# Moving 1.5 MB of one gradient store to four of the sixteen DMA engines in a one-query attention kernel

## The chip, the cores and the metric

The kernel runs on one core of one Trainium2 chip. The metric is the device time of one execution in microseconds. Before the change it is 646.4 us, the median of three runs (646.16 to 646.51). The profile of one execution has a span of 644.5 us at a mean granted TensorE clock of 0.600.

## The reference

It is attention with one query per head, forward and backward, for 32 heads, 8192 keys and a head size of 128, all bf16. The outputs are the attention result and the gradients of q, k and v.

```python
B, H, Sq, Skv, Dh = 1, 32, 1, 8192, 128
scores = jnp.einsum('bhqd,bhkd->bhqk', q, k) * q.shape[-1] ** -0.5
attn   = jax.nn.softmax(scores, axis=-1)
out    = jnp.einsum('bhqk,bhkd->bhqd', attn, v)
# out, and the gradients of q, k, v for a given grad_out (jax.vjp)
```

K and V of one head are 2 MB each, and so are dK and dV. The kernel has to read 134.23 MB and write 134.23 MB, and does little arithmetic with either.

## The kernel before

The kernel goes head by head. Every transfer that matters here is issued on the sync queue (SP). A head is kept with 128 partitions of 64 rows each, so that a full store or load is 128 packets of 16 KB. It has 16 landings, one for each DMA engine, and on the first engine the landings of successive transfers are 4.85 to 4.87 us apart (564.21, 569.08, 573.93, 578.80, 583.65 us), which is eight packets of 607 ns. K and V come in ahead of their use:

```python
def load_v(h):
    Vt[h] = vpool.tile([P, NT, D], BF16, tag="V", name="Vt")
    nc.sync.dma_start(Vt[h][:], rows_of(v, h, 0, 1))
```

dK and dV are outer products of one value for each key and one row. VectorE makes them in four quarters (`r` = 0 to 3) in a buffer `G` in SBUF; the store is issued after the last quarter, or in two halves for the first and the last head:

```python
def outer(h, which, r):
    # ... (cut: choice of the operands; Q = NT // 4)
    nc.vector.tensor_tensor(slots(G, r, 4)..., op=ALU.mult)      # shortened
    parts = 1
    if h == 0 or h == H - 1:
        parts = 2
    if r % (4 // parts) == 4 // parts - 1:
        c = r // (4 // parts)
        nc.sync.dma_start(rows_of(dst, h, c, parts), slots(G, c, parts))
```

`G` has two buffers for each of dK and dV, so a store has to land before the product of the head after the next one may overwrite it.

## Time and profile before

| What | Value |
|---|---|
| Time | 646.4 us |
| Span of the profile | 644.5 us |
| Busy: TensorE, VectorE, ScalarE | 75%, 78%, 28% |
| Bytes in bulk transfers, all on the sync queue's hardware queue | 268.47 MB |
| DMA rate with all engines busy | about 428 GB/s |
| Last landing of the last big store: first engine, last engine | 633.9 us, 643.22 us |

Three kinds of record are used. The page's row of slices cuts the span in 40 equal parts and gives the DMA engines' mean busy share in tenths and the GB/s. The view of stretches (windows) gives, for each stretch of time, the busy time and instruction count of TensorE, its weight loads, VectorE, ScalarE and GpSimd, then the granted TensorE clock, the DMA share and the GB/s. Below these lie the raw records: each DMA packet with its start, size and duration, and each increment of a semaphore. A store raises its semaphore once for each engine that takes part, when this engine's part has landed: 16 times for a full store. These "landings" show how far the engines are apart, though neither kind of record names the engine.

### The profile page before, as it was taken

What the parts mean: (1) busy time and instruction counts of PE and PEld (TensorE: products, weight loads), DVE (VectorE), ACT (ScalarE), POOL (GpSimd) and SP (SyncE); (2) the same over time, 40 slices, a digit from 0 to 9 for tenths busy, and PEclk for the clock granted to TensorE, in tenths of its full rate; (3) what the DMA queues carried; (4) which work ended last, traced back from release to release, by engine and by line L of the source; (5) the groups of instructions that cost most, each with busy time, mean ns of one, the idle gap of its engine ahead of it and who ended that gap; (6) DMA issues with size and microseconds to landing.
All of it is one profiled execution on the core that took longest, in us unless ns stands there. A gap on an engine that the chain in (4) does not pass through costs nothing.

```text
span 644.5 us, 20935 instructions
## 1 busy us (share of the span) xinstructions
PE 481.0 (75%) x9673; PEld 452.0 (70%) x9673; DVE 505.5 (78%) x653; ACT 183.5 (28%) x332; POOL 0.7 (0%) x6
## 2 busy tenths in 40 slices
PE   3898888886677877768777787667786777877780
PEld 2888888886677866768666777667785676866670
DVE  5989899867977779777788777797767977778860
ACT  2333333332233222233222332223322223222230
POOL 0000000000000000000000000000000000000000
PEclk9766666655666655666556666556655666655665
DMA  8999999999999999999999999999999999999985
GB/s 349 407 425 430 424 425 423 429 426 431 427 428 427 427 427 429 429 429 425 433 422 433 425 430 427 427 429 425 427 429 425 431 425 429 429 427 430 424 365 238
DMA packets 19718, 269.80 MB, mean 419 GB/s; under 512 B 2352, under 2 KB 2352, under 8 KB 2864
## 3 DMA queue, kind: packets, MB, share of 16 engines
q1 hardware_dynamic: 19584, 268.47, 98.2%
q8 instruction: 75, 1.23, 0.7%
q14 instruction: 11, 0.09, 0.0%
q10 hardware_dynamic: 48, 0.01, 0.0%
HBM read 134.23 MB, written 134.23 MB: 417 GB/s over the span
## 4 chain that ended last, share of the span: by engine, by line
DMA 59%; PE 21%; DVE 14%; ACT 2%; issue 1%; SPq 0%; DVEq 0%; ACTq 0%
DMA Kt<-in_k_dram 48%; DVE XK_sb L146 8%; PE T_ps L183 8%; DMA out_dram<-G_dv 5%; DMA out_dram<-G_dk 5%; PE s_ps L157 5%; DVE G_dk L210 4%; PE dp_ps L200 3%; PE m_ps L200 2%; PE dp_ps L195 2%; ACT XT_sb L185 1%; PE m_ps L294 1%; DVE G_dv L210 1%; PE s_ps L173 1%; DVE sm L163 1%
## 5 line engine op out<-in xcount | busy, mean ns | idle before, releaser
L210 DVE TENSOR_TENSOR G_dv<-p_rep,qd 128x2048 bf16<-128x2048 bf16 x128 | 148.2, 1221 | 90.3 <-DMA out_dram<-G_dv 84.6
L183 PE MATMUL T_ps<-ident_f,Vt 128*128 128x128 f32 x1024 | 203.4, 382 | 0.2 <-PE m_ps L294 0.2
L183 PEld LDWEIGHTS T_ps<-ident_f,Vt 128*128 128x128 f32 x1024 | 190.7, 210 | 0.2 <-issue 0.2
L185 ACT COPY XT_sb<-T_ps 128x1024 f32<-128x1024 f32 x128 | 128.6, 1013 | 129.3 <-PE T_ps L183 127.2
L210 DVE TENSOR_TENSOR G_dk<-ds_rep,qd 128x2048 bf16<-128x2048 bf16 x128 | 155.6, 1218 | 2.9 <-DMA out_dram<-G_dk 1.9
L146 DVE STREAM_TRANSPOSE XK_sb<-Kt 128x1024 f32<-128x1024 f32 x128 | 148.3, 1214 | 5.8 <-DMA Kt<-in_k_dram 4.7
L157 PEld LDWEIGHTS <-XK_sb 128*128 128x128 bf16 x2048 | 57.7, 104 | 90.7 <-DVE pdt L234 79.9
L157 PE MATMUL s_ps<-q_blk,XK_sb 128*128 128x4 bf16 x2048 | 59.7, 168 | 82.1 <-DVE pdt L234 72.1
L195 PE MATMUL dp_ps<-do_blk,XT_sb 128*128 128x2 bf16 x2048 | 66.7, 164 | 18.1 <-ACT XT_sb L185 18.1
L195 PEld LDWEIGHTS <-XT_sb 128*128 128x128 bf16 x2048 | 64.9, 102 | 20.7 <-ACT XT_sb L185 20.7
L200 PE MATMUL dp_ps<-ds_rep,Kt 128*128 128x1 bf16 x2048 | 64.1, 165 | 1.3 <-issue 1.0
L200 PEld LDWEIGHTS <-Kt 128*128 128x128 bf16 x2048 | 59.6, 104 | 6.8 <-issue 6.6
L244 ACT COPY dq_all<-dp_ps 128x1 f32<-128x1 f32 x32 | 5.1, 159 | 192.4 <-PE dp_ps L200 178.5
L200 PEld LDWEIGHTS <-Vt 128*128 128x128 bf16 x2048 | 57.7, 97 | 0.9
L200 PE MATMUL m_ps<-p_rep,Vt 128*128 128x1 bf16 x2048 | 56.9, 164 | 0.0
L294 PEld LDWEIGHTS m_ps<-rs,ones_f 128*128 128x128 f32 x64 | 16.0, 311 | 49.9 <-ACT e L293 49.9
L294 PE MATMUL m_ps<-rs,ones_f 128*128 128x1 f32 x64 | 18.8, 362 | 40.5 <-ACT e L293 40.5
L303 ACT ACTIVATE p_rep<-e,rinv 128x256 bf16<-128x256 f32 x32 | 16.3, 508 | 30.1 <-DVE rinv L301 30.1
L163 DVE TENSOR_TENSOR sm<-s_ps,in_quad 128x256 f32<-128x256 f32 x32 | 13.6, 424 | 11.1 <-PE s_ps L157 7.9
L229 ACT CAST qd<-s_ps 128x256 bf16<-128x256 f32 x32 | 11.9, 372 | 32.2 <-PE s_ps L225 32.2
L236 DVE SCALAR_TENSOR_TENSOR ds_rep<-dp_ps,pdt,p_s 128x256 bf16<-128x256 f32 x32 | 15.5, 484 | 5.2 <-PE dp_ps L195 2.4
L293 ACT ACTIVATE e<-s_ps,nbias 128x64 f32<-128x64 f32 x32 | 10.0, 313 | 31.8 <-DVE nbias L290 31.8
(44 smaller groups left out, 143.4 us busy)
## 6 DMA issues: line engine op xcount, KB each, us to landing
Vt<-in_v_dram SPq DMA_DIRECT2D x32, 2048.0 KB, 30.0
Kt<-in_k_dram SPq DMA_DIRECT2D x31, 2048.0 KB, 30.8
out_dram<-G_dv SPq DMA_DIRECT2D x30, 2048.0 KB, 34.6
out_dram<-G_dk SPq DMA_DIRECT2D x30, 2048.0 KB, 33.6
out_dram<-G_dv SPq DMA_DIRECT2D x4, 1024.0 KB, 15.0
out_dram<-G_dk SPq DMA_DIRECT2D x4, 1024.0 KB, 13.3
Kt<-in_k_dram SPq DMA_DIRECT2D x4, 512.0 KB, 5.1
out_dram<-fin_sb SPq DMA_DIRECT2D x2, 8.0 KB, 13.1
```

The costliest lines, as they stand in the source:

```text
L146: nc.vector.transpose(XK[h][:, :, :, u, :], slots(Kt[h], u, NCH).rearrange("p g d -> p (g d)").bitcast(F32).rearrange("p (g w j) -> p g w ...
L157: nc.tensor.matmul(out[:, g, :], lhsT=cols[:, g, c // 2, c % 2], rhs=q_blk[:, h, c, :], start=(c == 0), stop=(c == 2 * NB - 1), skip_group ...
L163: nc.vector.tensor_tensor(x["sm"][:], x["s"][:, 0:NT].rearrange("p (a g) -> p a g", a=NQ).unsqueeze(2) .to_broadcast([P, NQ, NCH, CH]), in ...
L183: nc.tensor.transpose(T_ps[:, i, :], words[:, m * P:(m + 1) * P], ident_f[:])
L185: nc.scalar.copy(X[:], T_ps[:])
L195: nc.tensor.matmul(st[h]["dp"][:, n:n + 2], lhsT=X[:, i, e2, :], rhs=do_blk[:, h, e2, :], start=(e2 == 0), stop=(e2 == 1), skip_group_chec ...
L200: nc.tensor.matmul(out_col, lhsT=Xt[:, n, :], rhs=rep[:, n, 0:1], start=(n == 0), stop=(n == NT - 1), skip_group_check=True)
L210: nc.vector.tensor_tensor(slots(G, r, 4).rearrange("p n (a b) -> p n a b", b=R), slots(rep, r, 4).unsqueeze(2).to_broadcast([P, Q, D // R, ...
L229: nc.scalar.copy(x["qd"][:].rearrange("p a d -> p (a d)"), x["s"][:, 256:512])
L236: nc.vector.scalar_tensor_tensor(out=x["ds"][:], in0=x["dp"][:, 0:NT].unsqueeze(2).to_broadcast([P, NT, R]), scalar=pdt[:], in1=x["p_s"][: ...
L294: nc.tensor.matmul(x["m"][:, 0:1], lhsT=ones_f[:], rhs=rs[:], start=True, stop=True, skip_group_check=True)
L303: nc.scalar.activation(x["p"][:], e[:].unsqueeze(2).to_broadcast([P, NT, R]), ACT.Copy, scale=rinv[:])
```

## The change

The intent is to even out the DMA engines at the end of the kernel. Nine of them end late and seven end early; the change takes work for one store from twelve engines and gives it to four. The first quarter of dV of head 30 (0.5 MB) still goes out on all 16 engines. The other three quarters (1.5 MB) go out as one store of 124 partitions and one of 4. The change counts on both using the same four engines. No trace before the change showed this. Their numbers, 0 to 3, are in no record and serve only as names: in e3 the landings of loads of 1, 2, 4 and 8 partitions tell the engines apart, and "engine 3" is one that takes part in a load of four partitions but not in one of two.

```diff
-        if r % (4 // parts) == 4 // parts - 1:
+        if h == H - 2 and which == "dv":
+
+            rows4 = dst[0, h].rearrange("(p n) d -> p n d", p=P)
+            if r == 0:
+                nc.sync.dma_start(rows4[:, :Q, :], G[:, :Q, :])
+            elif r == 3:
+                for lo, hi in ((0, P - 4), (P - 4, P)):
+                    nc.sync.dma_start(rows4[lo:hi, Q:, :], G[lo:hi, Q:, :])
+        elif r % (4 // parts) == 4 // parts - 1:
             c = r // (4 // parts)
             nc.sync.dma_start(rows_of(dst, h, c, parts), slots(G, c, parts))
```

## The prediction

> **What bounds the kernel now.** I read the row of 40 slices first, then the queues, the issues of the sync queue, the stretches of the last 40 us, and last the landing times.
>
> From the page (slices, then queues):
>
> ```profile
> DMA  8999999999999999999999999999999999999985
> GB/s 349 407 425 430 424 425 423 429 426 431 427 428 427 427 427 429 429 429 425 433 422 433 425 430 427 427 429 425 427 429 425 431 425 429 429 427 430 424 365 238
> ...
> q1 hardware_dynamic: 19584, 268.47, 98.2%
> q8 instruction: 75, 1.23, 0.7%
> q14 instruction: 11, 0.09, 0.0%
> ```
>
> The DMA engines are full from the second slice to the 38th at about 428 GB/s; no compute engine is over 78% busy. So the time is the bytes over the DMA rate, plus a tail in the last two slices (365 and 238 GB/s). 428 GB/s over 16 engines is 26.7 GB/s each. The packet records agree: a 16 KB packet takes 611 ns and the next begins 4 ns before it ends, so 607 ns each (27.0 GB/s); in the same way 8 KB costs 305 ns and 4 KB 155 ns.
>
> The sync queue's last issues in order of time (start us, us, engine, line, what):
>
> ```profile
> 594.00 0.33 SPq L220 DMA_DIRECT2D out_dram<-G_dk  x1
> 602.61 0.33 SPq L220 DMA_DIRECT2D out_dram<-G_dv  x1
> 614.52 0.33 SPq L220 DMA_DIRECT2D out_dram<-G_dk  x1
> 621.05 2.60 SPq L220 DMA_DIRECT2D out_dram<-G_dv  x2
> ...
> 627.72 2.60 SPq L220 DMA_DIRECT2D out_dram<-G_dk  x2
> ```
>
> These are dK of head 29, dV of head 30 (the store that is changed), dK of 30, the two halves of dV of 31 and of dK of 31. No load is left behind them. After 627.7 us nothing but stores remains:
>
> ```profile
> 612.00:616.00 4.00, 2.64 (x12) 2.33 (x12) 2.90 (x6) 1.07 (x4) 0.00 (x0) 0.50 0.74 311
> ...
> 636.00:640.00 4.00, 0.00 (x0) 0.00 (x0) 0.00 (x0) 0.00 (x0) 0.00 (x0) 0.50 0.55 232
> 640.00:645.00 5.00, 0.00 (x0) 0.00 (x0) 0.00 (x0) 0.00 (x0) 0.00 (x0) 0.50 0.09 37
> ```
>
> The last two columns are DMA share and GB/s. A share of 0.55 is about 9 of 16 engines busy: the engines do not end together, and 7 are done while 9 still work.
>
> The landing records say the same more sharply. A store raises its semaphore once for each of the 16 engines, so each has 16 landing times. For dK of head 29 the first comes at 607.96 us, six more 0.03, 0.18, 0.24, 0.50, 1.53 and 4.91 us later, then a gap, and nine from 12.73 to 15.43 us later. Early in the run all 16 lie within 0.6 us. The lag grows by about 1.5 us on one engine at each packet of queue 8 (takes about 1.02 us, and the packet behind it about 1.1 instead of 0.61). Followed packet by packet, these 75 fetches go round eight engines; the ninth late engine has none and falls behind slowly, by packets of 620 to 700 ns. The last landing of dK of 31 is at 633.9 us on the first engine and at 643.22 us on the last; the span ends at 644.5 us and the run counts 646.4. So the nine late engines set the end, and they never idle on the way.
>
> [...]
>
> **Which engines lead?** The records do not name them. Where two packets of different size or duration start in the same nanosecond, their order in the record is stable (one pair 12 times of 12), and in nearly all such pairs a leading engine stands before the late one without fetches, and this before the fetching ones. If the records are kept by engine number, the fetching ones are 8 to 15 and the leaders among 0 to 7. I take it that 0 to 3 lead; an inference, at some 88%.
>
> **The change part by part.**
>
> The computation is untouched: every instruction of the compute engines stays, in the same order. The sync queue gets three issues (128 x 4 KB after the first quarter, some 3.4 us earlier; 124 x 12 KB; 4 x 12 KB) for one. Nothing in the tail waits for dV of head 30: dV of 31 needs the buffer of dV of 29, dK of 31 that of dK of 29. So issue times stay.
>
> Twelve engines: they had 8 packets of 16 KB (8 x 607 = 4.86 us) of dV of 30 and now have 8 of 4 KB (8 x 155 = 1.24 us): minus 3.62 us each. The late ones have no idle time before the end, so all of it arrives: 643.22 - 3.62 = 639.6 us.
>
> Engines 0 to 3: 1.24 us plus 31 + 1 = 32 packets of 12 KB. At (305 + 607)/2 = 456 ns, an estimate between 8 and 16 KB, that is 14.59 us; together 15.83 instead of 4.86 us. A first engine free of dK of 29 at 607.96 ends dV of 30 at 623.8, dK of 30 (4.86) at 628.7, dV of 31 (16 x 305 = 4.88) at 633.5 and dK of 31 (4.88) at 638.4 us. Before, it idled between these and ended at 633.9: of the 10.97 us added, about 6.5 go into gaps. With the leaders' lags of 0 to 1.53 us they end at 638.4 to 639.9, beside the late ones' 639.6.
>
> Sum: the end moves from 643.2 to about 639.6 to 639.9, and 646.4 becomes 642.8 to 643.1: 0.5% faster. The size of 1.5 MB is just the balance of the two groups, so more should not be hoped for.
>
> **The rivals.**
>
> *A lagging leader is among 0 to 3.* One leader is 4.91 us late. On 0 to 3 it would end at 638.4 + 4.9 = 643.3: no change, 646.5. By count alone 4 in 7; the balance of the size speaks against it, so I give it less.
>
> *Shared ports.* [...] Two readers at one port, if each gets half, take 2 x 456 ns a packet: 14 us more at worst, end near 652, time 650 to 656; with three at one port, up to 664. [...] I give it 3 in 10.
>
> *The four engines are late ones.* Then all 10.97 us fall on the end: 654.2, time 657.4. One in ten.
>
> *The compute chain or the sync queue takes over.* The chain ends at 630 us with the last issue; a half of dK of 31 needs 2.44 us and the landing, so it cannot end before about 634. It leaves 5 us of room.
>
> **Range and chances.** The mechanism worked out gives 642.8 to 643.1; the rivals lie on the upper side alone, so I put the point a little above, at 643.6 us. Below, nothing can go under 639.6 - 643.2 by more than noise, hence 642.3. Above, the ports and the wrong engines could reach 664; 657 leaves out about one in ten. Faster by over 2% (under 633.5) would need more than the whole tail of the late engines: 1%. Slower by over 2% (over 659.3) is the worst of the port rival: 9%. Within 2%: 90%.
>
> **What would show it.** Right: the store of 124 partitions lands in about 16 to 20 us after its issue with 4 landings, its 12 KB packets take about 460 ns, the last stretch has nearly all 16 engines busy until 639 us and then falls off steeply, and the late engines end about 3.6 us sooner. Wrong by ports: 12 KB packets of 600 to 1300 ns and 16 KB ones well over 611 at the same time, and four engines alone at work after 641 us. Wrong by the engines' place: 12 KB packets at 460 ns, yet four engines alone to 654 us. Wrong altogether: 16 landings for the 124-partition store, and the time of before.

The sum: 643.22 - 3.62 = 639.6 us for the late engines, up to 639.9 for the four, with 646.4 - 643.2 = 3.2 us from the last landing to the time, so 642.8 to 643.1 us. But that just four engines take the 32 packets, and that the same four serve both stores, stands in it as an assumption, and so does the "port" of the rival: the word names a theory, that reads of SBUF by several engines can slow each other. No record shows a port.

## The result, and the profile after

The changed kernel takes 654.33 us, the median of four runs (653.93 to 654.78), against 646.28 us (646.16 to 646.51, four runs) for the kernel before. The ratio is 1.0124, with a 95% interval of 1.0107 to 1.0142. Ratios here are the mean time of one kernel's runs over that of the other's of the same rounds, so not quite the ratio of the medians that are quoted. The kernel became 1.2% slower.

The page's slices of the kernel after:

```profile
DMA  8999999999999999999999999999999999999992
GB/s 347 410 426 424 426 426 425 430 426 429 426 430 425 430 427 429 424 430 428 429 426 431 427 429 428 428 429 425 429 426 430 427 429 426 429 426 430 378 335 102
```

Up to the 37th slice nothing has changed (a slice is 16.3 us here and 16.1 before). The last three fall to 378, 335 and 102 GB/s (before: 424, 365 and 238), although the busy share stays at 90% or more in slices 38 and 39. The engines are busy and move less.

The sync queue's issues of the kernel after (start us, us, engine, line, what):

```profile
599.42 0.33 SPq L222 DMA_DIRECT2D out_dram<-G_dv  x1
602.83 0.82 SPq L225 DMA_DIRECT2D out_dram<-G_dv  x2
614.00 0.36 SPq L228 DMA_DIRECT2D out_dram<-G_dk  x1
620.87 2.68 SPq L228 DMA_DIRECT2D out_dram<-G_dv  x2
...
627.09 3.02 SPq L228 DMA_DIRECT2D out_dram<-G_dk  x2
```

These are the first quarter of dV of head 30, its two stores on four engines, dK of 30, and the halves of dV and dK of 31. Each comes within 0.7 us of its place before (602.61, 614.52, 621.05, 627.72). So the computation was not held up, and the loss came after the issues, on the DMA engines.

More stretches of the kernel before:

```profile
616.00:620.00 4.00, 4.00 (x37) 3.94 (x36) 1.34 (x2) 2.32 (x3) 0.00 (x0) 0.50 1.03 438
...
628.00:632.00 4.00, 0.00 (x0) 0.00 (x0) 1.96 (x2) 0.25 (x1) 0.00 (x0) 0.50 0.94 395
...
640.00:644.00 4.00, 0.00 (x0) 0.00 (x0) 0.00 (x0) 0.00 (x0) 0.00 (x0) 0.50 0.11 46
```

The same stretches, and the later ones, of the kernel after:

```profile
612.00:616.00 4.00, 2.70 (x14) 2.67 (x14) 2.38 (x5) 1.15 (x4) 0.00 (x0) 0.50 0.87 351
616.00:620.00 4.00, 4.00 (x59) 3.97 (x58) 1.52 (x2) 2.69 (x3) 0.00 (x0) 0.64 1.00 374
...
628.00:632.00 4.00, 0.00 (x0) 0.00 (x0) 1.33 (x2) 0.00 (x0) 0.00 (x0) 0.50 0.98 340
...
636.00:640.00 4.00, 0.00 (x0) 0.00 (x0) 0.00 (x0) 0.00 (x0) 0.00 (x0) 0.50 0.60 251
640.00:644.00 4.00, 0.00 (x0) 0.00 (x0) 0.00 (x0) 0.00 (x0) 0.00 (x0) 0.50 0.25 105
644.00:648.00 4.00, 0.00 (x0) 0.00 (x0) 0.00 (x0) 0.00 (x0) 0.00 (x0) 0.50 0.16 66
648.00:652.00 4.00, 0.00 (x0) 0.00 (x0) 0.00 (x0) 0.00 (x0) 0.00 (x0) 0.50 0.05 21
```

The last two columns, DMA share and GB/s, are to be read together. From 616 to 620 us all engines are busy in both kernels, yet they move 438 GB/s before and 374 after. From 628 to 632 us the share rises from 0.94 to 0.98 while the rate falls from 395 to 340. From 640 to 644 us the share is 0.25, which is 4 of 16 engines; then it falls to 0.05, which is one engine.

The packet records of the two new stores, worked out from the trace, say the same packet by packet:

```text
128 packets of 12 KB, mean 693 ns
  the 28 that start before 613.3 us          460 ns each
  the 39 that start from 613.3 to 619 us     mean 578 ns
  the 61 that start after 619 us             mean 872 ns, up to 1966 ns
16 KB packets in the same time               up to 1276 ns (before: up to 1019; most 611)
first 12 KB packet of the four engines       608.48, 608.74, 610.18, 613.99 us
```

And the landings, as the first time and the further ones after it:

```text
first quarter of dV30, 16 engines  608.82  +.04 .26 .37 .84 1.70 5.56 | nine from +12.84 to +17.10
124 partitions, 4 engines          628.73  +1.91 2.11 7.60
last half of dK31, before          633.91  +.01 .04 .08 .08 .10 .18   | nine from 640.14 to 643.22
last half of dK31, after           633.77  +.93 1.56 | nine from 637.99 to 640.85 | 643.89 647.33 647.43 651.48
```

Three things stand in these lines. The 124-partition store used four engines, as intended. The nine late engines end 2.2 to 2.4 us sooner than before. But the four engines now end last, and one of them much later than the others. This one starts its 12 KB packets about 5.5 us after the first and takes 22.5 us for 32 of them (613.99 to 636.45), where 32 x 456 ns would be 14.6 us. The 7.9 us lost there, added to the 643.3 us at which such an engine would end otherwise (the prediction's first rival), make 651.2; its part of the last half of dK of 31 lands at 651.48 us.

So two causes were in question: an engine among the four that is late on its own, and slow packets. The first theory for the slow packets is that engines which read SBUF at the same time slow each other ("shared ports"). The rivals were a cost of the split stores as such (small issues, the moved time of the first quarter, the writes to DRAM), and a simple wrong choice of engines.

### The profile page after: what moved, and what is told of

Same layout as the page of the kernel before. It is cut to its first block, busy times and chain, and to the rows that moved or that the text cites. A ratio compares the mean times of both kernels' runs of the same rounds, so it can differ in the third digit from the quotient of the medians.

```text
span 652.7 us, 20938 instructions
## 1 busy us (share of the span) xinstructions
PE 479.8 (74%) x9673; PEld 451.1 (69%) x9673; DVE 505.4 (77%) x653; ACT 183.8 (28%) x332; POOL 0.7 (0%) x6
## 4 chain that ended last, share of the span: by engine, by line
DMA 58%; PE 21%; DVE 14%; ACT 2%; issue 1%; SPq 0%; DVEq 0%; ACTq 0%
DMA Kt<-in_k_dram 53%; DVE XK_sb L146 9%; PE T_ps L183 7%; PE s_ps L157 5%; DMA out_dram<-G_dv 5%; PE dp_ps L200 3%; DVE G_dk L210 3%; PE m_ps L200 2%; PE dp_ps L195 2%; ACT XT_sb L185 1%; PE m_ps L302 1%; DVE G_dv L210 1%; PE s_ps L173 1%; DVE sm L163 1%; ACT e L301 1%
## 5 line engine op out<-in xcount | busy, mean ns | idle before, releaser
L302 PEld LDWEIGHTS m_ps<-rs,ones_f 128*128 128x128 f32 x64 | 16.1, 312 | 49.9 <-ACT e L301 49.9
L311 ACT ACTIVATE p_rep<-e,rinv 128x256 bf16<-128x256 f32 x32 | 16.3, 508 | 30.0 <-DVE rinv L309 30.0
```

What stands on the lines that cost most here:

```text
L302: nc.tensor.matmul(x["m"][:, 0:1], lhsT=ones_f[:], rhs=rs[:], start=True, stop=True, skip_group_check=True)
L311: nc.scalar.activation(x["p"][:], e[:].unsqueeze(2).to_broadcast([P, NT, R]), ACT.Copy, scale=rinv[:])
```

## The experiments

Ten kernels were run, in three batches; those of a batch ran on one chip together with the kernel before. The edits of e1, e2, e6, e8, e9 and e10 are shown against the changed kernel, those of e3, e4, e5 and e7 against the kernel before.

### e1: the same split in time, but on sixteen engines

```diff
-                for lo, hi in ((0, P - 4), (P - 4, P)):
-                    nc.sync.dma_start(rows4[lo:hi, Q:, :], G[lo:hi, Q:, :])
+                nc.sync.dma_start(rows4[:, Q:, :], G[:, Q:, :])
```

> The early first quarter is kept, but the other three quarters of dV of head 30 go out as one store of 128 partitions on all 16 engines. All theories that blame the four engines (shared ports, or a late engine among 0 to 3) expect the time of before, 646.3 us within 0.5 us, because each engine carries the same bytes. A theory that blames the split in time or the extra issue expects a good part of the 8 us to stay.

Measured: 646.2 us (646.02 to 646.31) against 646.4 (646.1 to 646.59), ratio 0.9998 (0.9981 to 1.0014). The first quarter sent early, and the packets of 12 and 4 KB, cost and win nothing. Whatever the change does comes from the use of four engines.

### e2: the four engines' stores read from DRAM in place of SBUF (wrong result)

```diff
+                src4 = v[0, h].rearrange("(p n) d -> p n d", p=P)
                 for lo, hi in ((0, P - 4), (P - 4, P)):
-                    nc.sync.dma_start(rows4[lo:hi, Q:, :], G[lo:hi, Q:, :])
+                    nc.sync.dma_start(rows4[lo:hi, Q:, :], src4[lo:hi, Q:, :])
```

As many bytes go to the same addresses in the same packets, on four engines again; only the source is not in SBUF, so these two stores read none of it. These two stores no longer wait for `G` and are issued 3 us sooner (599.82 for 602.83 us), but their first packet starts no sooner than in the changed kernel (609.24 for 608.48 us), since the engines reach them only then.

> Wrong result on purpose: the two transfers on engines 0 to 3 read the same rows of v in DRAM instead of the tile in SBUF, [...] engines, bytes, packet sizes and destination stay. Shared SBUF ports: all 128 packets of 12 KB take about 460 ns, and the end is set only by the late leader (608 + 5.6 + 15.8 + 14.6 = 644.0 us for its last landing), time about 647 us. Contention outside the SBUF ports [...]: packets stay near the mean of 693 ns of the changed kernel and the time near 654 us.

Measured: 646.59 us (646.46 to 646.8), ratio 1.0003 (0.9988 to 1.0018). Two stretches of its profile:

```profile
616.00:620.00 4.00, 4.00 (x24) 3.94 (x24) 0.98 (x1) 2.03 (x2) 0.00 (x0) 0.50 1.01 430
...
640.00:644.00 4.00, 0.00 (x0) 0.00 (x0) 0.00 (x0) 0.00 (x0) 0.00 (x0) 0.50 0.04 19
```

At the same busy share as in the changed kernel the engines move 430 GB/s in place of 374. All 128 packets of 12 KB take exactly 460 ns, so 456 ns from one to the next, as the prediction estimated. The nine late engines end between 636.9 and 639.9 us, 3.3 us sooner than before. The last landing of dK of 31, at 643.26 us, belongs to one engine alone: its part of the 124-partition store landed 4.35 us after that of the first engine.

This splits the loss in two. Reading from SBUF, in place of DRAM, costs 654.33 - 646.59 = 7.7 us. What is left of the change without that cost is worth nothing, because one of the four engines starts about 4.5 us late and so ends where the late engines ended before.

### e3: small loads that show where the late engines stand

```diff
+        if h == H - 4:
+            for n_ in (1, 2, 4, 8):
+                pr = consts.tile([n_, D], BF16, name="probe%d" % n_)
+                nc.sync.dma_start(pr[:], k[0, 0, 0:n_, :])
```

The trace shows 1, 2, 4 and 8 landings. Each is to show how far its engine is behind when the load comes to it.

> The kernel before with four tiny loads at head 28, of 1, 2, 4 and 8 partitions, which should run on engine 0, on 0 and 1, on 0 to 3 and on 0 to 7. Their landings show how far each of these engines is behind. My inference (0 to 7 hold the seven leaders and the slow one; the eight fetching engines are 8 to 15): the load of 8 partitions lands within about 1 us on six engines, about 5 us later on one, and 12 to 15 us later on one. Late leader is engine 0, as the groups of four packets in the trace of after suggest: the load of 1 partition lands about 5 us after the first of the others. Were fetching engines among 0 to 3, the load of 4 partitions would have landings 12 us late.

Measured (one run, 647.36 us, state unknown, result right):

```text
partitions  first landing   further ones after it, us
1           569.12
2           569.31          1.25
4           569.32          .17 1.43 4.91
8           569.24          .26 .43 1.69 5.18 13.33 13.48 14.17
```

The spread is that of a big transfer: the one that begins to land at 569.08 us in the kernel before has six more landings up to 1.51 us later, but for one at 4.91 us, and nine from 11.23 to 13.86 us later. The sets of engines also seem to contain each other, since the lags recur, 0.18 to 0.19 us later from load to load: 569.12, 569.31, 569.49, 569.67; then 570.56, 570.75, 570.93; 569.32, 569.50; and 574.23, 574.42. So the engines can be named by the smallest load in which they appear: 0 for one partition, 1 for two, 2 and 3 for four, 4 to 7 for eight.

Engine 0 is early, engine 1 is 1.25 us behind it, and engine 2 or 3 is the leader that is 4.9 us behind. Of engines 4 to 7, three are among the late ones. The lags of the load of four (0, 0.17, 1.43, 4.91 us) are nearly those of the first 12 KB packets of the changed kernel (0, 0.26, 1.70, 5.51 us), so these are taken to be the same four engines. They do lead, but they hold the one leader that lags. And three late engines among these eight do not fit the numbering by which the prediction placed all the engines that fetch instructions at 8 to 15, as it counted only one late engine without fetches. The guess of the expectation that engine 0 might be the lagging one was a miss.

The probes were not free. Their four issues took 10.57 us in the sync queue, which waited for landings between them; the issues and two of the sync queue's waits (us in total, times, longest):

```profile
552.78 10.57 SPq L280 DMA_DIRECT2D probe<-in_k_dram  x4
```

```profile
SPq L280 <- DMA out_dram<-G_dv: 4.6, 1, 4.6
...
SPq L280 <- DMA Kt<-in_k_dram: 4.6, 1, 4.6
```

### e4: the two stores alone at the end (wrong result)

```diff
     result(dq_all, out_1)
+    Q = NT // 4
+    late = kpool.tile([P, NT, D], BF16, tag="K", name="late")
+    nc.sync.dma_start(late[:, Q:, :], rows_of(v, H - 1, 0, 1)[:, Q:, :])
+    rows4 = out_3[0, H - 1].rearrange("(p n) d -> p n d", p=P)
+    for lo, hi in ((0, P - 4), (P - 4, P)):
+        nc.sync.dma_start(rows4[lo:hi, Q:, :], late[lo:hi, Q:, :])
```

> Wrong result on purpose: the kernel before, then, after everything has landed, a load of 1.5 MB on all engines and a store of it as 124 and 4 partitions x 12 KB with nothing else running. Shared ports, [...] about half to nine tenths of the packets take near 0.9 us, and the store takes 22 to 28 us. Contention with the other engines' traffic elsewhere: 32 packets of 460 ns, 14.6 us.

Measured (one run, 669.78 us, state unknown): the packets begin at 647.6 us, and the four engines are done between 664.7 and 666.7 us, so they take 17 to 19 us where 32 packets at 456 ns would take 14.6. Two stretches:

```profile
648.00:652.00 4.00, 0.00 (x0) 0.00 (x0) 0.00 (x0) 0.00 (x0) 0.00 (x0) 0.50 0.24 68
...
660.00:664.00 4.00, 0.00 (x0) 0.00 (x0) 0.00 (x0) 0.00 (x0) 0.00 (x0) 0.50 0.25 104
```

With nothing else in flight, the same four engines move 68 GB/s at first and 104 at the end. Of 128 packets 87 take 460 to 490 ns, and 28 take over 1.5 times 460, up to 1136. The direction is that of the theory that the reads of SBUF slow each other; the size, put at 22 us or more, is smaller. (No run shows which partitions an engine reads when.) The packets fit four engines that soon fall out of step and then rarely meet: their mean is 718 ns for those that start before 651 us and 468 ns from 659 to 663 us. Alone, the stores lose 2.5 to 4.5 us. The larger loss in the changed kernel, 7.9 us on the engine that ended last, is put down to the stores of the other engines, whose packets were slowed at the same time.

### e5: which sets of partitions collide (wrong result)

```diff
+    late = kpool.tile([P, NT, D], BF16, tag="K", name="late")
+    nc.sync.dma_start(late[:], rows_of(v, H - 1, 0, 1))
+    rows4 = out_3[0, H - 1].rearrange("(p n) d -> p n d", p=P)
+    for _ in range(2):
+        for lo, hi, step in ((0, 4, 1), (0, 16, 4), (0, 128, 32), (0, 64, 16)):
+            nc.sync.dma_start(rows4[lo:hi:step], late[lo:hi:step])
```

Each store has four partitions of 16 KB, in four packets; only the choice of partitions differs.

> Wrong result on purpose: the kernel before, then a load, and behind it, with nothing else running, stores of 4 partitions x 16 KB on engines 0 to 3, one packet each, from four sets of partitions, the sets twice over: 0,1,2,3; 0,4,8,12; 0,32,64,96; 0,16,32,48. [...] about 2.4 us for the first set, 0.61 for the second, 1.2 us for the third and the fourth. If an SBUF read is bounded by the engine alone: 0.61 us in all sets.

Measured (one run, state unknown):

```text
partitions       one 16 KB packet, ns
0 1 2 3          2171 to 2347
0 4 8 12         612 to 614
0 32 64 96       1141 to 1246
0 16 32 48       1049 to 1153
```

As many bytes in as many packets take 612 to 614, 1049 to 1246 or 2171 to 2347 ns a packet, according to the partitions read: 1.7 to 2.0 times the shortest for the last two sets, and 3.5 to 3.8 times for four neighbouring partitions. It looks as if all four packets of the first set waited for each other, none of the second, and pairs in the last two; which pairs, the run does not show. (The rows that are written in DRAM change with the partitions too. That they are not the cause is not tested alone, but in e2 the store of four neighbouring rows took 460 ns a packet as all others did.) The times come out near the expected 2.4, 0.61, 1.2 and 1.2 us; which partitions share what, these four sets do not single out. The trace of the kernel before had no such case; this run shows it for reads of SBUF.

### e6: a third of the bytes, the last quarter alone on four engines

```diff
-            if r == 0:
-                nc.sync.dma_start(rows4[:, :Q, :], G[:, :Q, :])
+            if r == 2:
+                nc.sync.dma_start(rows4[:, :3 * Q, :], G[:, :3 * Q, :])
             elif r == 3:
                 for lo, hi in ((0, P - 4), (P - 4, P)):
-                    nc.sync.dma_start(rows4[lo:hi, Q:, :], G[lo:hi, Q:, :])
+                    nc.sync.dma_start(rows4[lo:hi, 3 * Q:, :], G[lo:hi, 3 * Q:, :])
```

> Only the last quarter (0.5 MB) of dV of head 30 goes to engines 0 to 3, as packets of 4 KB. Twelve engines lose 1.2 us; engine 3 or 2, the late leader, gets 3.7 us more than before without sharing and some 8 us with it, and ends at 637 to 641 us, before the late engines. Shared ports: [...] the time is 645.1 to 646.3 us. Without sharing: 645.1 us.

Measured: 645.3 us (644.91 to 645.61) against 646.22 (645.93 to 646.59), ratio 0.9985 (0.9971 to 0.9998). The 128 packets of 4 KB have a mean of 183 ns; 113 of them are near 159, and 13 over 1.5 times that. Here the late engines are spared 8 x 155 ns = 1.24 us, and the time falls by 0.9 us. With this smaller amount the packets collide seldom (13 of 128), and the lagging engine of the four lands its part of the last half of dK of 31 at 636.8 us, ahead of the nine late ones (639.1 to 641.7).

### e7: a load of V in place of a store on four engines

```diff
-        nc.sync.dma_start(Vt[h][:], rows_of(v, h, 0, 1))
+        if h == H - 1:
+            half = NT // 2
+            rows4 = rows_of(v, h, 0, 1)
+            nc.sync.dma_start(Vt[h][:, :half, :], rows4[:, :half, :])
+            for lo, hi in ((0, P - 4), (P - 4, P)):
+                nc.sync.dma_start(Vt[h][lo:hi, half:, :], rows4[lo:hi, half:, :])
+        else:
+            nc.sync.dma_start(Vt[h][:], rows_of(v, h, 0, 1))
```

> dV is stored as before; instead the second half (1 MB) of the load of V of head 31 goes to engines 0 to 3, as packets of 8 KB. When the leaders come to it, the other engines write into SBUF only for K of head 31. [...] packets stay near 309 ns but for those that meet that load; the late engines are spared 2.43 us, and engines 0 to 3 get 7.3 us, which the late leader can bear (608.0 + 5.1 + 7.3 and 19.5 us of stores is 639.9): time 644.0 us, 2.4 less than before. [...] packets take about 600 ns and the time is 646 to 650 us.

The two cases are: the loads and the other engines' traffic do not slow each other (644.0 us), or they do (646 to 650 us). Measured: 646.35 us (646.28 to 646.89, five runs), ratio 1.0004 (0.9991 to 1.0016); the hoped-for 644.0 was missed. One stretch of the kernel before, then of this one:

```profile
600.00:604.00 4.00, 3.36 (x102) 3.27 (x99) 3.82 (x5) 1.35 (x3) 0.00 (x0) 0.88 1.04 438
```

```profile
600.00:604.00 4.00, 3.65 (x83) 3.57 (x79) 2.93 (x3) 1.13 (x3) 0.00 (x0) 0.69 1.04 367
```

All engines are busy in both, but the rate is 367 in place of 438 GB/s. The 8 KB packets take up to 966 ns in place of 309. The late engines were still loading K of head 31 at first (up to 605.26 us) and later the first half of V, and 16 KB packets of that time took up to 1284 ns (before, from 599 to 606 us, at most 985), so here the loads took longer together, as the stores did in the changed kernel. What they share is not shown: no run separates it for loads. What then came late was K of 31, on the late engines: it landed at 605.26 us, before at 602.73. VectorE's first instruction on K waited for that, as the lines of the kernel before and of this one show:

```profile
602.76 4.63 DVE L146 STREAM_TRANSPOSE XK_sb<-Kt 128x1024 f32<-128x1024 f32 x4 [0.18 <-DMA Kt<-in_k_dram]
```

```profile
605.29 4.62 DVE L153 STREAM_TRANSPOSE XK_sb<-Kt 128x1024 f32<-128x1024 f32 x4 [2.36 <-DMA Kt<-in_k_dram]
```

The chain that ended last in this run goes through this landing, and the last issues moved back (dK of 31 from 627.72 to 629.51 us). V of 31 itself landed at 614.04 us, only 0.4 us later than before, and nothing waited for it. What the late engines gained was given back through the computation.

### e8: three engines and DRAM, to leave out the lagging engine and the reads of SBUF (wrong result)

```diff
-            if r == 0:
-                nc.sync.dma_start(rows4[:, :Q, :], G[:, :Q, :])
+            if r == 1:
+                nc.sync.dma_start(rows4[:, :2 * Q, :], G[:, :2 * Q, :])
             elif r == 3:
-                for lo, hi in ((0, P - 4), (P - 4, P)):
-                    nc.sync.dma_start(rows4[lo:hi, Q:, :], G[lo:hi, Q:, :])
+                src4 = v[0, h].rearrange("(p n) d -> p n d", p=P)
+                for lo, hi in ((0, P - 5), (P - 5, P)):
+                    nc.sync.dma_start(rows4[lo:hi, 2 * Q:, :], src4[lo:hi, 2 * Q:, :])
```

The store of 123 partitions has three landings, the one of 5 has five.

> Wrong result on purpose: 1 MB of dV of head 30 from DRAM as in e2, now as 123 and 5 partitions, on engines 0 to 2 (and one packet each on 0 to 4). Probe and trace say that engine 3 or 2 is the late leader. If it is engine 3: the three end at 637.5 us plus their lag of at most 1.5, the late engines are spared 2.43 us and set the end at 640.8: time 643.9 us. If it is engine 2, its end is 637.5 + 5 = 642.5 us and the time 645.6 us.

Measured: 644.26 us (644.01 to 644.34), ratio 0.9968 (0.9953 to 0.9983). The landings:

```text
first half, 16 engines    610.25  +.05 .36 .54 .64 1.42 5.23 | nine from +12.80 to +15.79
123 partitions            622.80  +.55 1.41
5 partitions              615.77, 623.12, 623.67, 624.53, 626.38
```

The engine that lags by 5.2 us in the first line is missing in the second and is there in the third (615.77 is 610.25 + 5.23 plus one 8 KB packet of 0.305). The three engines of the second line recur in the third, each 0.32 us later (623.12, 623.67, 624.53). So the 123-partition store leaves out the lagging leader; it is engine 3. The fifth landing, 626.38, fits the last of the late ones (610.25 + 15.79 + 0.305 = 626.35), so the fifth engine is a late one. And with both causes removed the mechanism works: 8 packets of 8 KB less on the late engines are 2.4 us, and the time falls by 2.0.

### e9: the first quarter on four engines

```diff
             if r == 0:
-                nc.sync.dma_start(rows4[:, :Q, :], G[:, :Q, :])
-            elif r == 3:
                 for lo, hi in ((0, P - 4), (P - 4, P)):
-                    nc.sync.dma_start(rows4[lo:hi, Q:, :], G[lo:hi, Q:, :])
+                    nc.sync.dma_start(rows4[lo:hi, :Q, :], G[lo:hi, :Q, :])
+            elif r == 3:
+                nc.sync.dma_start(rows4[:, Q:, :], G[:, Q:, :])
```

> The first quarter (0.5 MB) of dV of head 30 on engines 0 to 3 as packets of 4 KB, the rest on 16 engines: as e6, but the leaders reach these packets 3.7 us earlier, at 608 us, when the late engines load V of head 31 [...]. [...] nearly all 128 packets take 159 ns, the late engines are spared the full 1.21 us, time 645.0 us. If the timing does not matter, as in e6: up to a quarter of the packets over 200 ns, time 645.3 us.

Measured: 645.13 us (645.02 to 645.44, five runs) against 646.42 (645.96 to 646.76, nine runs), ratio 0.9979 (0.9965 to 0.9993), with the right result. Of the 128 packets of 4 KB, 121 take 159 ns, and 7 take over 200 ns, where e6 had 13. The two expected times, 645.0 and 645.3 us, lie within the spread of the runs, so the time does not tell them apart; the packets lean to the first. It is 0.2% faster than the kernel before and, by the medians of different rounds, 1.4% faster than the changed one, the best right version that was found; e6 lies beside it.

### e10: the same for heads 29 and 30

```diff
-        if h == H - 2 and which == "dv":
+        if h in (H - 3, H - 2) and which == "dv":
```

(The rest is as in e9.)

> The same for heads 29 and 30. The late engines are spared 2 x 1.21 us, engines 0 to 3 get 3.7 us for each: the late leader ended at 636.8 us in e6 and would end at 640.5, the late engines at about 640.8. [...] with both quarters meeting loads at the other engines: time 643.9 us, 0.4% under before. If the first of the two meets stores, packets near 300 ns and a time of 644.5 to 645.5 us.

Measured: 648.34 us (647.73 to 648.85, five runs), ratio 1.003 (1.0018 to 1.0043): a miss, slower where faster was expected. Two readings offered themselves. The first is the sync queue. Its waits over the whole run (us in total, times, longest), four of those on landings, which e9 does not have:

```profile
SPq L225 <- DMA out_dram<-G_dk: 9.2, 2, 4.8
...
SPq L228 <- DMA Vt<-in_v_dram: 4.4, 1, 4.4
...
SPq L223 <- DMA out_dram<-G_dv: 3.2, 1, 3.2
SPq L223 <- DMA Kt<-in_k_dram: 3.2, 1, 3.2
```

The issue of the rest of dV of head 30 in e9, and then in e10:

```profile
602.95 0.36 SPq L225 DMA_DIRECT2D out_dram<-G_dv  x1
```

```profile
608.13 0.35 SPq L225 DMA_DIRECT2D out_dram<-G_dv  x1
```

With two more stores in flight the queue waited for older landings, and this issue came 5.2 us later. Why it had to wait for these is not shown; no run varied it. But the wait did not set the end. The landings of the lagging engine, picked by the lag that it has in each store, run without a gap to the last one ("at the lone rate" is what its packets would take without collisions, at 155, 305, 456 and 607 ns each):

```text
                              lagging engine lands at   it takes           at the lone rate
dK of 28, all its packets     599.02
124 partitions, head 29       605.89                    6.87               31 x 155 = 4.81
...
dK of 29                      619.55
124 partitions, head 30       626.93                    7.38               4.81
4 partitions, head 30, rest of
  dV30, dK30, dV31, dK31      645.42                    18.49              0.16 + 3.65 + 4.86 + 4.88 + 4.88 = 18.43
```

It was still at older work when the late issue came at 608.13 us. In e9 it ended at 637.1 us. One more head gives it 32 packets of 4 KB in place of 8, which is 3.7 us; the two stores of 124 partitions took 4.6 us more than at the lone rate, of which the one store of e9 had 0.7. That makes 644.7 of the 645.4 us of its last landing; the rest is not accounted for. The 4 KB packets agree: their mean is 194 ns in e10 and 177 in e9, and 32 of 256 take over 240 ns. The nine late engines ended at 641.09 us, 2.1 us sooner than before. So the lagging engine has no room for a second head: it ended 2.2 us after the 643.2 us of the kernel before. The expectation had left the collisions out.

## Why the prediction was wrong

**What held.** The stores of 124 and of 4 partitions went out on four engines each, as their four landings show. The spacing of 12 KB packets, estimated at 456 ns between two measured sizes, was exact where nothing collides (e2). The issue times of the tail stayed within 0.7 us. The late engines set the end before the change, and where they alone are relieved the time follows: 1.3 us in e9 for 1.24 worked out, 2.0 in e8 for 2.4. The four engines do lead, which was put at 88%, though the argument for it was wrong: three of the late engines are among the eight of the load of 8 partitions (e3). So this was right by luck. (One issue did move: the small last store of dq came at 636.39 in place of 630.41 us, after a wait of 6.2 us for a landing of dV. It landed right behind dK of 31, as before, so this did not set the end.)

**The first step that failed: "With the leaders' lags of 0 to 1.53 us they end at 638.4 to 639.9, beside the late ones' 639.6."** The seven leaders at 607.96 us had lags of up to 4.91 us, and the prediction took the four without the large one. It reasoned that the size of 1.5 MB "is just the balance of the two groups", which is an argument from the intent and not from the trace. The lagging one is among the four (4.91 us behind in e3, 5.51 at the first 12 KB packet of the changed kernel). It has to carry as much as each of the other three, so it would have ended at 643.3 us. Where the two stores read no SBUF it did end at 643.26 (e2), and the time was 646.59 us. So this one step turns the forecast of 642.8 to 643.1 into no gain at all. It was the prediction's first rival, 646.5 us, which it gave less than the 4 in 7 that counting alone gave.

**The second step that failed: engines 0 to 3 get 32 packets of 12 KB at "(305 + 607)/2 = 456 ns".** The size was right where nothing collides (460 ns a packet in e2), but here the mean was 693 ns. This is the second rival, given 3 in 10 with 650 to 656 us. The time, 654.33, lies in its range, but partly by luck: the rival had up to 14 us for the doubled packets and no lag, where about 7.5 us of slow packets and about 5 us of lag were measured. The cost of the slow packets is the difference to e2, 7.7 us; the engine that ended last lost 7.9 us in its 32 packets. Typical slow packets took 900 to 971 ns (32 of the 61 after 619 us), about twice 456; in e5 the sets that took about twice as long took 1049 to 1246 ns for 612. That the reads of SBUF are the cause is shown by e2 (four engines, as many bytes, same destinations, no SBUF read: every packet 460 ns). That the time of such stores goes by the partitions they read is shown by e5, with nothing else running (same sizes, other partitions: 612 to 614, 1049 to 1246 or 2171 to 2347 ns). The conflict also hit the others: the late engines were spared 2.2 to 2.4 us in place of the 3.62 of the prediction and the 3.3 of e2.

The two failures add up. The slow packets hit all four engines alike: their 32 packets took 22.5 us on the late one and 22.0 us on the mean of the other three, in place of 14.6. These three ended at 643.9 to 647.4 us, already after the 643.2 of the kernel before. So the slow packets alone would have made the change a loss, about 650.6 us (an estimate: 647.4 and the 3.2 us between last landing and time before), and the late start of the lagging engine carried it to 654.3.

**What stays open.** Which engine read which partitions at each moment is not in the records, and no run gave the four engines other partitions beside the full traffic. From its 13th packet on the lagging engine shows groups of four, three slow and one nearly free (701, 900, 915, 562; 900, 902, 959, 488; 962, 940, 966, 589 ns and so on); why is not shown. Nor is it shown why this engine lags, or which engines fetch the instructions. A fetch (a packet of queue 8, "instruction", 75 of them) took about 1.02 us, and the packet behind it about 1.1 in place of 0.61, so a fetch costs its engine about 1.5 us. By the prediction's count the 75 fetches go round eight engines, which is about 14 us each (an estimate: 75 x 1.5 / 8), and the nine late engines were 12.7 to 15.4 us behind the first by the landing of dK of 29. But the ninth is as late without fetches, so they are not the whole cause.

## What to carry to other kernels

In this kernel a transfer on few engines was not free for being on engines with idle time. It read SBUF beside the other engines' stores, and slowed both itself (12 KB packets of 900 to 971 ns in place of 460) and those stores (16 KB packets from 611 to as much as 1276 ns). Before work is moved to "engines that have room", measure the room of each, for instance with loads of 1, 2, 4 and 8 partitions whose landings tell the engines apart, and plan by the worst of them. Here the sign of the conflict was a high busy share of the DMA engines at a falling rate (share 1.00 at 374 GB/s, before 1.03 at 438).
